# Block-sparse attention feeding a SoLU MLP on one core: mask chain, first columns of Q, spare matmuls and weight loads of the opening rearranged, all priorities set anew

## The chip, the cores and the metric

The kernel runs on one core of a Trainium2 chip. The metric is the device time of one execution in microseconds (us); a kernel's figure is the median of several runs. TensorE is written PE, VectorE DVE, ScalarE ACT, GpSimd POOL, SyncE (which issues most DMAs) SP. Single runs of one and the same kernel here spread by 1 to 1.5% either way. Part of that is PE's clock: in traces of b_rows and of the kernel before, whose instructions up to there are the same, PE came to its full rate at 4.4 and at 16.0 us. Every run therefore comes with the mean clock that was granted to PE.

## The reference, cut to what matters

```python
# q, k, v: (4 batches, 8 heads, 768 tokens, 64); block = 32, so 24 blocks
scores = scale * np.matmul(q, k.transpose(0, 1, 3, 2))
mask = np.abs(blk_i - blk_j) <= 1
mask = mask | (blk_i == 0) | (blk_j == 0) | (blk_i == n_blocks - 1) | (blk_j == n_blocks - 1)
for qb in range(n_blocks):
    for kb in sampled_blocks[qb]:                      # 3 random blocks per row
        mask[qb*32:(qb+1)*32, kb*32:(kb+1)*32] = True
attn = softmax(np.where(mask, scores, -1e9))           # [cut: written out]
x = (attn @ v)                                         # -> (3072 tokens, 512)
h = x @ w_in                                           # (512, 1024)
solu = h * softmax(h)
ln = (solu - mean) / np.sqrt(var + 1e-6) * g_ln
out = ln @ w_out                                       # (1024, 512)
```

## The kernel before

The mask is added inside the score matmul. Rows 64 to 87 of `kT` and `qT` hold a block selector and the block mask, so a score is one matmul over 88 rows, and `exp` of a blocked score is 0. Heads go in pairs; a *unit* is one pair with one query tile of 256: three groups of four score matmuls (one ACT exponential each), then 24 PV matmuls, then a DVE division into `x`. A finished query tile of `x` is transposed by a DMA, multiplied by `w_in`, put through ACT, DVE and POOL, transposed again and multiplied by `w_out`.

All instructions are first put into one list by a planner in the host program: each operation has a priority `due`, and the planner places the ready operation with the smallest one. What comes out is the in-order instruction stream of each engine. So a priority, or an estimated time, that changes in the opening can move every later instruction.

```python
key = (t if late else now, o.due)          # in the planner: earliest, then smallest due
if best is None or key < best[0]:
    best = (key, o, max(t, now))
# [cut]
for i in range(7):                         # 28 spare matmuls for the clock, all at the start
    w = op("PE", 0.43, warm_mm, [m1], due=-60, take="m", after=[w] if i else [])
# [cut: POOL and DVE build selq (24x768), static, anyeq, maskq]
def mask_mm(o):                            # all 768 columns of the mask rows
    for g in range(2):
        nc.tensor.matmul(sbank[o.slot]...[0:NB, g*512 : g*512 + S//2], maskq,
                         selq...[:, g*(S//2) : (g+1)*(S//2)], start=True, stop=True)
# [cut: ACT copies them to qT rows 64..87 of head 0, DVE from there to head 1]
rest = {nm: op("POOL", 0.84, lambda o, t=t: nc.gpsimd.dma_start(      # pairs 1 to 3
    out=t[0][D:DM, 1:NPR]..., in_=t[0][D:DM, 0:1]....broadcast_to([NB, NPR - 1, 2 * S])),
    rows[nm], due=-2059, load=0.8) for nm, t in (("k", kT), ("q", qT))}
w_in_load = op("POOL", 0.82, lambda o: nc.gpsimd.dma_start(
    out=w_in_sb, in_=moe_w_in...), [stage[("k", 0, 2)]], due=-2000, load=6.35)
for i in range(3):                         # w_out in float32, into buffers that are free yet
    w_out_load.append(op("SP", 0.5, lambda o, i=i: nc.sync.dma_start(out=hold[i], ...),
        due=-43.4 + 0.1 * i, load=2.3, after=[stage[("v", 0, 3)]]))
# [cut]
wo = [op("DVE", 0.39, lambda o, c=c: nc.vector.tensor_scalar(         # 8 scalings w_out * g
    out=w_out_sb[:, c, :], in0=w_out_f[c], scalar1=g_sb[:, c:c+1], scalar2=None,
    op0=ALU.mult), [w_out_load[c // 3], gc], due=26) for c in range(KF)]
```

The 24x768 mask rows of the first pair are written once by engines, and then copied to the other three pairs (`rest`) by two POOL DMAs. No `w_out` matmul, and no transpose ahead of one, can start before the eight scalings `wo` are done.

The softmax here doesn't subtract the row's maximum and nothing guards it: scores larger than these inputs give would overflow.

Of the kernel before, what the change touches and what calls it, by code (L numbers as in the profile page):

```python
# [8 lines left out]
BF16 = mybir.dt.bfloat16  # L9
I32 = mybir.dt.int32  # L10
AX = mybir.AxisListType
ALU = mybir.AluOpType
# [3 lines left out]
INF = float("inf")  # L16

# [36 lines left out]
class Plan:  # L54
# [24 lines left out]
    def run(self):  # L79
# [10 lines left out]
        while len(order) < len(self.ops):  # L90
# [17 lines left out]
            self.free[o.eng] = t + o.us  # L108
            o.start = t
            o.seen = t + o.us + SEEN[o.eng]  # L110
# [4 lines left out]
            elif o.load is not None and o.eng != "SP":  # L115
                o.seen = t + 2.8 + o.load + 0.6 * min(o.load, max(0.0, self.dma_free - t - 1.5))
                self.dma_free = max(self.dma_free, t + 1.5) + o.load
            elif o.load is not None:
                self.dma_free = max(self.dma_free, t + 1.0) + o.load
                o.seen = self.dma_free + 1.3  # L120
                self.landed.append(self.dma_free)
                if len(self.landed) > 6:
                    self.free["SP"] = max(t + o.us, self.landed[-7])
# [20 lines left out]
def kernel(  # L144
# [33 lines left out]

    NST, NKB, NEX, NX, NE, NSO, NSOT, NXT, NOT = 4, 3, 9, 6, 2, 3, 3, 2, 3
# [101 lines left out]
    for b in range(B):  # L281
# [6 lines left out]
    m1 = op("DVE", 0.15, lambda o: nc.vector.memset(onesf, 1.0), due=-99)  # L288
    mid = op("POOL", 0.15, lambda o: nc.gpsimd.memset(ident, 0.0), due=-98)
    mids = op("POOL", 0.35, lambda o: nc.gpsimd.affine_select(  # L290
        out=ident, in_=ident, compare_op=ALU.not_equal, fill=1.0, base=0, channel_multiplier=1,
        pattern=[[-1, P]]), [mid], due=-97)

    idf = op("DVE", 0.1, lambda o: nc.vector.tensor_copy(out=identf, in_=ident[0:KF, 0:KF]), [mids], due=-80)

    def warm_mm(o):
        for _ in range(4):
            nc.tensor.matmul(bank(o)[:, 0:P], onesf, onesf, start=True, stop=True)

    for i in range(7):  # L300
        w = op("PE", 0.43, warm_mm, [m1], due=-60, take="m", after=[w] if i else [])
        w.last_of.append((w, "m"))
        w.held["m"][0] = 1


# [6 lines left out]
    def chain(first, steps, due):  # L312
        last = op("POOL", 0.12, first, due=due)
        for us, fn in steps:
            last = op("POOL", us, fn, [last], due=due)
        return last

    def sel(t, us, fill, base, cm, pat, cmp=ALU.is_ge):
# [4 lines left out]
            due=-96)  # L323
    stat = chain(lambda o: nc.gpsimd.memset(static, 0.0),
                 [sel(static, 0.2, -NEG, 1, -1, [[1, NB]]), sel(static, 0.2, -NEG, 1, 1, [[-1, NB]]),
                  sel(static, 0.2, 0.0, -1, 1, [[0, NB]]), sel(static, 0.2, 0.0, NB - 2, -1, [[0, NB]]),
                  (0.1, lambda o: nc.gpsimd.memset(static[:, 0:1], 0.0)),
                  (0.1, lambda o: nc.gpsimd.memset(static[:, NB - 1 :], 0.0))], -94)
    sqs = chain(lambda o: nc.gpsimd.memset(selq, 1.0),
                [sel(selq, 1.05, 0.0, 0, -BLK, [[1, NCH], [NCH, P]]),  # L330
                 sel(selq, 1.05, 0.0, BLK - 1, BLK, [[-1, NCH], [-NCH, P]])], -93)
    last = op("DVE", 0.1, lambda o: nc.vector.memset(anyeq, 0.0), due=-95)
# [8 lines left out]
    def mask_mm(o):  # L341
        for g in range(2):
            nc.tensor.matmul(sbank[o.slot].rearrange("p a b -> p (a b)")[0:NB, g * 512 : g * 512 + S // 2], maskq,
                             selq.rearrange("b c p -> b (c p)")[:, g * (S // 2) : (g + 1) * (S // 2)],
                             start=True, stop=True)

    mmm = op("PE", 0.4, mask_mm, [mq, sqs], due=-2088, take="sh")
    rows = {"k": [], "q": []}
    for hh in range(2):
        rows["k"].append(op("DVE", 0.3, lambda o, hh=hh: nc.vector.tensor_copy(  # L350
            out=kT[0][D:DM, 0, hh, :], in_=selq.rearrange("b c p -> b (c p)")), [sqs], due=-2087 if hh == 0 else -60))
        rows["q"].append(op("ACT" if hh == 0 else "DVE", 0.75 if hh == 0 else 0.3, lambda o, hh=hh: (
            nc.scalar.copy(out=qT[0][D:DM, 0, 0, :].rearrange("p (g n) -> p g n", g=2),
                           in_=sbank[mmm.slot].rearrange("p a b -> p (a b)").rearrange(
                               "p (g n) -> p g n", g=2)[0:NB, :, 0 : S // 2]) if hh == 0 else
            nc.vector.tensor_copy(out=qT[0][D:DM, 0, 1, :], in_=qT[0][D:DM, 0, 0, :])),
            [mmm] if hh == 0 else rows["q"][:1], due=-2087 if hh == 0 else -60,
            last_of=[mmm] if hh == 0 else []))
    rest = {nm: op("POOL", 0.84, lambda o, t=t: nc.gpsimd.dma_start(
        out=t[0][D:DM, 1:NPR].rearrange("p a h q -> p a (h q)"),  # L360
        in_=t[0][D:DM, 0:1].rearrange("p a h q -> p a (h q)").broadcast_to([NB, NPR - 1, 2 * S])),
        rows[nm], due=-2059, load=0.8) for nm, t in (("k", kT), ("q", qT))}
    vones = [op("POOL", 0.15, lambda o, i=i: nc.gpsimd.memset(va[i][:, :, :, D : D + 1], 1.0),
                due=-70 if i == 0 else 0) for i in range(2)]


    w_in_load = op("POOL", 0.82, lambda o: nc.gpsimd.dma_start(
        out=w_in_sb, in_=moe_w_in.rearrange("(c p) f -> p c f", p=P)), [stage[("k", 0, 2)]], due=-2000, load=6.35)
    w_out_load = []
    for i in range(3):  # L370
        w_out_load.append(op("SP", 0.5, lambda o, i=i: nc.sync.dma_start(
            out=hold[i], in_=moe_w_out.rearrange("(c p) d -> p c d", p=P)[:, 3 * i : min(3 * i + 3, KF)]),
            due=-43.4 + 0.1 * i, load=2.3, after=[stage[("v", 0, 3)]]))
    gt = op("PE", 0.1, lambda o: nc.tensor.matmul(bank(o)[:, 0:KF], g8, identf[0:KF, 0:KF], start=True, stop=True),
            [g_load, idf], due=-60, take="m")
    gc = op("DVE", 0.1, lambda o: nc.vector.tensor_copy(out=g_sb, in_=bank(gt)[:, 0:KF]), [gt], due=-60,
# [11 lines left out]
    def prepare(b, pr, due):  # L388
        i = b % 2
        first = b == 0 and pr == 0  # L390
        got = {0: [], 1: []}
        for nm, st, cb, dst in (("k", kst, kb, kT), ("q", qst, qb, qT)):
# [23 lines left out]
            ca = tp0 = None  # L416
            where = "sh" if first else "m"
            at = pair16 if where == "sh" else lambda o: bank(o, BF16)
            for part in range(2 if first else 1):
                cols = slice(part * D, part * D + D) if first else slice(0, P)  # L420
# [13 lines left out]
                def tp(o, at=at, ca=ca, cols=cols, tokens=tokens, tp0=tp0, part=part):  # L434
                    t = at(tp0 or o)[0 : cols.stop - cols.start, part * 1024 : part * 1024 + S]
# [4 lines left out]
                t = op("PE", NCH * 0.056, tp, [c_, mids], due=due, take=None if tp0 else where,  # L440
                       last_of=[ca], after=[tp0] if tp0 else [])
                tp0 = tp0 or t
                for hh in (part,) if first else (0, 1):
                    def cp(o, at=at, dst=dst, hh=hh, tp0=tp0, first=first):
                        r = 0 if first else hh * D
                        d_ = dst[i][0:D, pr, hh, :]
                        s_ = at(tp0)[r : r + D, (1024 * hh if first else 0) : (1024 * hh if first else 0) + S]
                        (nc.scalar.copy if o.eng == "ACT" else nc.vector.tensor_copy)(out=d_, in_=s_)
# [228 lines left out]
```

## Time and profile before

| what | where it is read | value |
|---|---|---|
| time | runs | 217.17 us (216.26 to 218.54) |
| span of the profiled run | page | 216.2 us |
| first score, first exponential | timeline | 8.74, 9.81 us |
| scores wait for the second pair's mask row | timeline | 1.85 us, until 19.05 |
| first `w_in` matmul, first `w_out` matmul | timeline | 45.88, 56.89 us |
| `w_out` scalings on DVE | timeline | 29.57 to 34.2 us |
| full clock from | transposes' durations | 16.0 us |

How to read a timeline line: start, duration, engine, source line, operation, output and input, shapes, how many instructions were merged and, in brackets, how long the engine had been idle and what ended that wait.

### The profile page before, as it was taken

How to read it: one execution, taken by the hardware profiler on the slowest of the kernel's cores; microseconds unless marked ns; L12 is line 12 of the kernel's file. 1: busy time of each engine (PE TensorE's matmuls, PEld its weight loads, DVE VectorE, ACT ScalarE, POOL GpSimd, SP SyncE). 2: the span in 40 equal slices, each digit the busy share in tenths (PEclk: the TensorE clock that was granted, in tenths of full speed). 3: DMA queues.
4: the chain of work that ended last, by engine and by line, in shares of the span. 5: the costliest groups of instructions: out<-in, count | busy, mean ns of one | idle time of the engine just before them, and what ended most of it. 6: DMA issues, size and time to landing. Idle time of an engine off the chain costs nothing.

```text
span 216.2 us, 5660 instructions
## 1 busy us (share of the span) xinstructions
PE 203.1 (94%) x2228; PEld 142.9 (66%) x2228; DVE 152.3 (70%) x358; ACT 164.9 (76%) x198; POOL 63.8 (29%) x135
## 2 busy tenths in 40 slices
PE   7996899899999999999988999999999999999992
PEld 6685787677767767777765677677766555764440
DVE  6554685048495888765965769976687799879991
ACT  3576799969999999999895996999887655934200
POOL 8431011313337063434140632342102211121121
PEclk9997899699999999999999999999999999999999
DMA  5999999997999999998999999995744436705822
GB/s 164 302 254 237 265 395 219 183 235 177 247 243 300 224 188 311 256 303 179 205 210 314 156 279 269 200 184 97 100 107 73 115 97 149 195 5 107 232 97 99
DMA packets 72639, 43.09 MB, mean 199 GB/s; under 512 B 55444, under 2 KB 67740, under 8 KB 72612
## 3 DMA queue, kind: packets, MB, share of 16 engines
q1 hardware_dynamic: 71904, 41.23, 84.2%
q0 software_dynamic: 656, 1.49, 3.5%
q8 instruction: 17, 0.28, 0.6%
q14 instruction: 10, 0.08, 0.1%
q10 hardware_dynamic: 52, 0.00, 0.0%
HBM read 23.07 MB, written 6.29 MB: 136 GB/s over the span
## 4 chain that ended last, share of the span: by engine, by line
PE 64%; DMA 15%; ACT 8%; DVE 5%; SPq 4%; issue 2%; POOL 0%; POOLq 0%; ACTq 0%; DVEq 0%
PE sbank L471 19%; PE mbank L589 16%; PE sbank L543 16%; PE mbank L488 11%; ACT ex L478 8%; DMA qst<-in_q_dram 8%; SPq L265 3%; DMA kb<-kb 3%; DMA qb<-qb 2%; DMA vst<-in_v_dram 2%; PE mbank L518 1%; DVE kT L407 1%; DVE bn L563 1%; DVE eso L556 1%; DVE qT L407 1%
## 5 line engine op out<-in xcount | busy, mean ns | idle before, releaser
L478 ACT ACTIVATE ex<-sbank 128x1024 bf16<-128x1024 f32 x144 | 137.6, 1037 | 14.3 <-PE sbank L471 13.6
L471 PE MATMUL sbank<-qT,kT 88*128 88x256 bf16 x576 | 87.7, 282 | 4.3 <-ACT ex L478 2.1
L471 PEld LDWEIGHTS <-kT 88*128 88x128 bf16 x576 | 54.8, 100 | 29.9 <-issue 7.5
L543 PE MATMUL sbank<-w_in_sb,xT 128*128 128x512 bf16 x192 | 52.5, 379 | 0.0
L488 PEld LDWEIGHTS <-ex 128*128 128x128 bf16 x1152 | 45.5, 100 | 6.2 <-DVE x L502 1.3
L589 PE MATMUL mbank<-w_out_sb,eso 128*128 128x512 bf16 x192 | 48.0, 379 | 1.6 <-DMA eso<-eso 1.1
L488 PE MATMUL mbank<-va,ex 128*128 128x65 bf16 x1152 | 47.3, 196 | 0.8 <-DVE x L502 0.7
L552 ACT ACTIVATE eso<-sbank 128x1024 bf16<-128x1024 f32 x24 | 24.8, 1035 | 21.2 <-issue 11.4
L556 DVE SCALAR_TENSOR_TENSOR eso<-sbank,eso 128x1024 bf16<-128x1024 f32 x24 | 29.3, 1221 | 7.6 <-ACT eso L552 7.5
L563 DVE BATCH_NORM_STATS2 bn<-eso 128x6 f32<-128x512 bf16 x48 | 30.8, 683 | 0.3
L499 DVE RECIPROCAL r<-mbank 128x4 f32<-128x4 f32 x48 | 8.6, 179 | 30.0 <-PE mbank L488 29.5
L589 PEld LDWEIGHTS <-eso 128*128 128x128 bf16 x192 | 17.9, 98 | 17.6 <-DMA eso<-eso 1.2
L570 POOL TENSOR_SCALAR mv<-se,mv 128x1 f32<-128x1 f32 x24 | 6.9, 289 | 76.3 <-DVE mv L566 71.2
L543 PEld LDWEIGHTS <-xT 128*128 128x128 bf16 x192 | 18.0, 98 | 10.1
L599 DVE TENSOR_SCALAR ot<-mbank,rs 128x512 f32<-128x512 f32 x24 | 17.9, 747 | 5.7 <-POOL qb L397 2.3
L502 DVE TENSOR_TENSOR x<-mbank,r 128x256 bf16<-128x256 f32 x48 | 19.9, 415 | 0.9
L454 POOL CAST va<-vst 128x768 bf16<-128x768 f32 x16 | 13.4, 837 | 18.9 <-DMA vst<-in_v_dram 18.9
L574 POOL TENSOR_TENSOR rs<-mv,neg_half 128x1 f32<-128x1 f32 x24 | 13.6, 566 | 12.9 <-DVE ot L599 11.7
L568 POOL TENSOR_TENSOR se<-se 128x1 f32<-128x1 f32 x24 | 4.7, 195 | 28.0 <-ACT eso L552 28.0
L397 POOL CAST kb<-kst 128x768 bf16<-128x768 f32 x12 | 10.2, 853 | 7.8 <-DVE r L499 6.2
L560 DVE TENSOR_SCALAR eso<-eso,mu 128x1024 bf16<-128x1024 bf16 x24 | 11.6, 483 | 0.2
L407 DVE COPY qT<-qb 64x768 bf16<-64x768 bf16 x24 | 10.1, 422 | 2.0 <-DMA qb<-qb 1.7
(64 smaller groups left out, 90.2 us busy)
## 6 DMA issues: line engine op xcount, KB each, us to landing
vst<-in_v_dram SPq DMA_DIRECT2D x16, 384.0 KB, 12.7
out_dram<-ot SPq DMA_DIRECT2D x24, 256.0 KB, 3.7
kst<-in_k_dram SPq DMA_DIRECT2D x15, 384.0 KB, 5.8
qst<-in_q_dram SPq DMA_DIRECT2D x15, 384.0 KB, 4.7
w_in_sb<-in_moe_w_in_dram POOLq DMA_DIRECT2D x1, 1024.0 KB, 13.9
kT<-in_moe_w_out_dram SPq DMA_DIRECT2D x1, 768.0 KB
qT<-in_moe_w_out_dram SPq DMA_DIRECT2D x1, 768.0 KB
eso<-in_moe_w_out_dram SPq DMA_DIRECT2D x1, 512.0 KB
```

Of the source, the lines that this page charges most:

```text
L407: nc.vector.tensor_copy(out=dst[i][0:D, pr, hh, :], in_=half(cb[ca.slot], 1)[hh * D : hh * D + D, :]),
L471: nc.tensor.matmul(s[:, m, :], kT[i][0:DM, pr, hh, jc * P : (jc + 1) * P], qT[i][0:DM, pr, hh, t * TW : (t + 1) * TW], start=(m % 2 == 0), ...
L478: exs.append(op("ACT", act_us(1024), lambda o, so=so: nc.scalar.activation(out=exb[o.slot], in_=sbank[so.slot], func=ACT.Exp, scale=scale) ...
L488: nc.tensor.matmul(acc[:, qt, hh, :], exb[exs[n].slot][:, m, qt * P : (qt + 1) * P], va[i][:, 2 * pr + hh, jc, :], start=(n + m + qt == 0) ...
L502: nrm = op("DVE", 0.39, lambda o: nc.vector.tensor_tensor(out=xb[x_of[(b, t)].slot][:, :, 2 * pr * D : (2 * pr + 2) * D].rearrange("p a (h ...
L543: nc.tensor.matmul(h[:, f * 512 : (f + 1) * 512], xTb[xp.slot][:, a, c, :], w_in_sb[:, c, f * 512 : (f + 1) * 512], start=(c == 0), stop=( ...
L552: se = op("ACT", act_us(d_ff) + 0.22, lambda o, h0=h0: nc.scalar.activation(out=eb[o.slots["e"]], in_=pair(h0), func=ACT.Exp, accum_out=se ...
L556: so = op("DVE", 1.29, lambda o, h0=h0, se=se: nc.vector.scalar_tensor_tensor(out=sob[o.slot], in0=pair(h0), scalar=1.0, in1=eb[se.slots[" ...
L563: bn = op("DVE", 2 * 0.64, lambda o, so=so: [nc.vector.bn_stats(out=bnb[o.slot][:, f], in_=sob[so.slot][:, f * 512 : (f + 1) * 512]) for f ...
L574: rs = op("POOL", 0.55, lambda o, mv=mv: nc.gpsimd.tensor_tensor(out=rsb[o.slot], in0=mvb[mv.slot][:, 0:1], in1=neg_half, op=ALU.pow), [q2 ...
L589: nc.tensor.matmul(bank(o0 or o), sotb[st.slot][:, f, :], w_out_sb[:, f, :], start=(f == 0), stop=(f == KF - 1))
L599: nc.vector.tensor_scalar(out=otb[o.slot], in0=bank(o0), scalar1=rsb[rs.slot], scalar2=None, op0=ALU.mult)
```

## The change

Its intent: start ACT's exponentials earlier and let PE reach and keep its full clock. The mask chain on POOL becomes shorter, by moving memsets to DVE. The mask matmul, the mask-row copies and Q's first copy are split by columns, so that the first query tile (256 columns) does not wait for the rest. Spare matmuls (44 instead of 28) are single ones, to be put into PE's gaps. `w_in` is loaded in two pieces behind the Q of the fourth pair, and `w_out` behind the first piece. All priorities, and some of the planner's estimates, are new.

```diff
-    for i in range(7):
-        w = op("PE", 0.43, warm_mm, [m1], due=-60, take="m", after=[w] if i else [])
+    def warm_mm(o):
+        nc.tensor.matmul(mbank[1][:, 3 * P : 4 * P], onesf, onesf, start=True, stop=True, ...)
+    for i in range(NWARM):                                  # 44
+        op("PE", 0.0535, warm_mm, [m1], due=1e7)
# [cut: memsets from POOL to DVE]
+    mmm = op("PE", 0.11, mask_mm, [mq, sqs], due=-2088, take="sh")        # columns 0..255
+    mmr = op("PE", 0.22, lambda o: mask_mm(o, mmm), [mq, sqs], due=-2079, after=[mmm])
+    qrow = {(0, 0): qrow_op("ACT", 0.36, 0, 0, TW, ps(0, TW), [mmm], -2087, [mmm]),
+            (1, 0): qrow_op("DVE", 0.36, 1, 0, TW, ps(0, TW), [mmm], -2079.6, [mmm])}
+    qrow[(0, 1)] = qrow_op("DVE", 0.62, 0, TW, S, ps(512, 1024), [mmr], -2078, [mmm])
# [cut]
-    w_in_load = op(... out=w_in_sb ..., [stage[("k", 0, 2)]], due=-2000, load=6.35)
+    w_in_load = [op(... out=w_in_sb[:, c : c + 2] ..., [stage[("q", 0, 3)]], due=-2000 + c, load=3.2)
+        for c in (0, 2)]
-            due=-43.4 + 0.1 * i, load=2.3, after=[stage[("v", 0, 3)]]))
+            due=-43.4 + 0.1 * i, load=2.3, deps=w_in_load[:1], after=[stage[("v", 0, 3)]]))
# in prepare(): K and Q of the first head are transposed into one PSUM tile of two banks
+                tp0 = shared_tp if shared and nm == "q" else None
+                off = 1024 if tp0 else 0
# [cut: Q's copies of the first pair split at column 256; new A, F, Q, SHIFT]
```

## The prediction

> **What bounds the kernel now.** I read the page first, then stretches of engine time, then the order of the first 30 us, the DMA issues and the chain of waits. On the page I want the bounding engine and where it is not full.
>
> ```profile
> PE 203.1 (94%) x2228; PEld 142.9 (66%) x2228; DVE 152.3 (70%) x358; ACT 164.9 (76%) x198; POOL 63.8 (29%) x135
> PE   7996899899999999999988999999999999999992
> ACT  3576799969999999999895996999887655934200
> ```
>
> TensorE (PE) is busy for 94% and full nearly everywhere after slice 9 (5.4 us each), so from about 50 us on the kernel is bound by PE. Before that PE's digits flatter it: busy is not full rate. The next view has columns start:end, length, busy time (instructions) of PE, weight loads, DVE, ACT, POOL, then granted clock, DMA share, GB/s.
>
> ```profile
> 9.20:12.60 3.40, 3.40 (x21) 2.59 (x20) 1.55 (x4) 2.05 (x2) 0.62 (x1) 1.00 1.08 275
> 16.00:19.40 3.40, 1.55 (x26) 1.32 (x24) 2.17 (x6) 1.70 (x2) 0.00 (x0) 1.00 1.07 236
> 19.40:22.80 3.40, 3.40 (x28) 2.73 (x26) 1.50 (x3) 2.56 (x3) 0.83 (x1) 0.50 1.11 252
> 36.50:39.90 3.40, 2.40 (x17) 1.54 (x16) 0.30 (x1) 3.40 (x5) 0.83 (x1) 1.00 1.46 134
> 39.90:43.30 3.40, 3.08 (x46) 2.76 (x45) 0.00 (x0) 3.07 (x4) 0.83 (x1) 0.50 0.88 215
> ```
>
> A half-full stretch (16.0 to 19.4, 36.5 to 39.9) is each time followed by one at a clock of 0.50. The column shows 1.00 ahead of 16 us, but the instructions there say otherwise: six transposes take 0.85 us until 15 us and 0.50 us at 16.7. So PE runs at half rate from the start to 16.0 us, and twice more.
>
> The timeline (start, duration, engine, line, operation, count, idle time before it) shows what the first scores wait for:
>
> ```profile
> 3.36 1.17 POOL L319 TENSOR_SCALAR_AFFINE_SELECT selq<-selq 24x768 bf16<-24x768 bf16 x1
> 6.34 0.16 DVE L337 SCALAR_TENSOR_TENSOR maskq<-anyeq,static 24x24 bf16<-24x24 f32 x1
> 6.56 0.81 PE L343 MATMUL sbank<-selq,maskq 24*24 24x384 bf16 x2
> 7.40 0.79 ACT L353 CAST qT<-sbank 24x768 bf16<-24x768 f32 x1
> 8.74 2.74 PE L471 MATMUL sbank<-qT,kT 88*128 88x256 bf16 x12
> 9.81 1.02 ACT L478 ACTIVATE ex<-sbank 128x1024 bf16<-128x1024 f32 x1 [0.81 <-PE sbank L471]
> ...
> 19.05 1.54 PE L471 MATMUL sbank<-qT,kT 88*128 88x256 bf16 x8 [1.85 <-DMA qT<-qT]
> ```
>
> The mask chain (POOL's selects, DVE's maskq, the mask matmuls, ACT's copy of 768 columns, then Q's own copy) releases the first score at 8.74. At 19.05 the second pair of heads waits for its mask row, copied by a POOL DMA that was issued at 10.09. Next, the DMA issues (size, issue to landing) and the longest piece of the chain of waits within the first 60 us:
>
> ```profile
> w_in_sb<-in_moe_w_in_dram POOLq DMA_DIRECT2D x1, 1024.0 KB, 13.9
> qT<-qT POOLq DMA_DIRECT2D x1, 216.0 KB, 8.8
> 8.54 16.96 DMA qst<-in_q_dram
> ```
>
> The Q of the fourth pair is issued at 8.54 and lands at 25.50: w_in, issued at 13.81, is in flight from then to 27.7 and shares the engines with it. The first matmul that uses w_in starts only at 45.88. The chain of attention is late because a weight comes too early.
>
> **What the Trainium skill says.** "TensorE: Matmul & The Clock Gate", Part 1 (The HAM clock gate): the idle state is half rate, and about 3.4 us of sustained work releases it, in windows that do not start with the kernel. The trace agrees: the two 0.50 stretches are 3.4 us long, and full rate comes at 16.0. Part 4 (PE-mode transpose) says that transposes do not count as busy for the gate; that fits a PE that was busy from 5 to 12.6 us and stayed cold, but this trace does not isolate it. "DMA: Bandwidth & Descriptors", Issuing engines are not separate DMA queues: transfers from all queues run on the same 16 engines and interleave; the landing at 25.5 agrees. Same page, Anatomy of one DMA: a POOL DMA costs some 2.0 us plus bytes/436 GB/s, that is 2.5 us for the mask row. The trace differs, 8.8 us, and decides.
>
> **The change part by part.**
>
> *Mask chain.* Four memsets move from POOL to DVE (selq's is 0.73 us on POOL), and POOL runs one short list: iota 0.14, four selects of static at about 0.2, two small memsets at 0.17, ident 0.28, two selects of selq at 0.86 (the undisturbed one): 3.3 us. It starts near 1.1 us, so selq ends at about 4.6, against 4.53 now: no gain there. But static ends near 2.5 instead of 5.52, so maskq comes at about 4.3 instead of 6.50 and the mask matmul is released by selq.
>
> *Column parts.* The first mask matmul has 256 columns, cold about 0.4 us against 0.81. ACT's copies of 256 instead of 768 columns should cost about 0.36 each, estimated from 0.79 for 768 with a third of the columns and a fixed part of 0.15. Chain: 4.7 + 0.4 + 0.2 + 0.36 + 0.36 and handovers gives a first score at about 6.4 to 6.8. I take 6.6, that is 2.1 us earlier. The second score needs the other head of Q, on which ACT waited until 6.75; with cast 0.5, transposes 0.85 and a copy of 0.3 it starts near 8.6. So ACT gets one exponential early and then a gap of about 0.5.
>
> *Spare matmuls.* 44 instead of 28, one by one, without a dependency on each other. Cold ones take 0.107 us, 4.7 us in all, and fill PE from about 1.1 to 6 us or later, interleaved with transposes. I expect full rate somewhere between 6 and 9 us instead of 16.0. Scores before 16 us (24 matmuls, 5.7 us cold) would take 2.6.
>
> *DMA order.* w_in goes behind Q of pair 3 and w_out behind half of w_in. The bulk data up to that Q is 4.3 MB plus 0.4 MB of mask rows; at 164 GB/s for the first 5.4 us (0.89 MB) and then about 275, it lands near 20 us (estimate) instead of 25.5. V of pair 3 follows near 21.5 instead of 27.5. w_in then lands near 30, still ahead of its use.
>
> *Mask row of pairs 1 to 3.* Issued after ACT's and DVE's parts of one head, at about 8 us instead of 10.09; with the same 8.8 us it lands at about 17, not 18.9. The first pair's two units last six exponentials, to about 14. A stall of 1 to 2 us remains unless scores of the third query tile fill it.
>
> *The sum, on ACT's path.* From 9.81 to 42.97 ACT does 31 exponentials. Twelve of them in a row took 11.13 us, 0.93 each, so 31 need 28.8 us; the other 4.4 us were waits. Afterwards: first one at 7.6, 28.8 of work, about 2.0 of waits (0.5 for the second head, 1.5 for the mask row) give 38.4 instead of 43.0: 4.6 us earlier. From there both kernels have the same remaining work, PE-bound, so the shift reaches the end. PE also loses the cold stretch from 39.9 to 43.3 (1.7 us of work), if FFN matmuls fill the gaps between scores that made it; the new priorities put the first w_in matmuls early. I count 1.4 us for that and take off 0.6 for w_in's second half coming later than planned. Gain: 4.6 + 1.4 - 0.6 = 5.4 us, and 217.2 - 5.4 = 211.8.
>
> As a ceiling: up to 50 us PE did 142 score matmuls at 0.109 us, 264 PV matmuls at 0.031, 8 of w_in at 0.216 and eight sets of transposes at 0.34, together 28.1 us of full-rate work, so 21.9 us are lost. With attention bound by ACT from 7.6 to 33 us (PE work of about 2.05 us per unit of three exponentials, 2.8 us), some 13 us of loss cannot go. The most to be had is thus about 9 us.
>
> **The rivals.** *First: the mask row keeps the old rhythm.* The POOL DMA may land at 18 to 19 us anyway, since it is now 144 pieces of half the size. Then pair 1 starts as before, PE idles for over half a window, goes cold again, and only what the earlier loads save later (waits of 0.47, 1.00 and 0.21 us between 21.7 and 28.2) is won, with a little of the filling: about 215. For it speaks the 8.8 us; against it that the second Q part is no longer in its way.
>
> *Second: a transfer takes the place of the one removed.* TensorE executes in order. If w_in or w_out land later than the new order assumes (13.9 us for 1 MB here), the first FFN matmul stands in PE's queue and blocks the scores behind it: 214 to 217. Against it: x of the first query tile is not complete until near 30 us anyway.
>
> *Third: all priorities were set anew.* The full stretch from 60 to 200 us, which now loses only 1.9 us of idle time, may get better or worse by 1 to 3 us, as may the tail, where PE is 4.3 us idle in the last 16. *Fourth: everything works*, FFN work fills PE from 33 us, and 208 to 209 comes out.
>
> **Range and chances.** Centre 211.8; 208.3 to 215.5 should hold it 8 times in 10: the low end is the ceiling of 9 us, the high end the first rival. Faster by over 2% means below 212.8. I give that 0.62, within 2% 0.36, slower 0.02, because nothing on the path gets longer except through the third rival.
>
> **What would show it.** Right: first score near 6.6 us and first exponential near 7.6; six transposes at 0.5 us before 10 us; Q of pair 3 landing near 20; the 31st exponential ending near 38.4; the first w_in matmul well ahead of 45.9; PE full after that. Wrong: a wait on the mask row at 18 us or later; a 0.50 clock stretch between 10 and 25 us; PE waiting on w_in or w_out; a first part that is 5 us earlier with the gain gone at 60 us, or lost between 60 us and the end.

## The result, and the profile after

The changed kernel took 225.52 us (median of 4 runs, 223.30 to 226.68), beside 217.62 us for the kernel before on the same chip (4 runs). It is slower. The ratio is 1.033 (95% interval 1.023 to 1.044). A ratio here is the mean time of one kernel's fast runs over that of the other's fast runs of the same rounds, so it is not quite the ratio of the medians quoted; a run counts as fast when it is within 1.5% of the fastest run of its kernel. A later set of rounds with the unaltered kernel gave 224.28 us and 1.037 (1.032 to 1.042).

On the page of the kernel after, the lines that answer to the first two fences of the prediction are these (busy times, and tenths in 40 slices, here of 5.6 us):

```profile
PE 203.1 (91%) x2216; PEld 142.8 (64%) x2244; DVE 153.7 (69%) x365; ACT 164.5 (74%) x198; POOL 63.6 (29%) x133
PE   6897986899799999999698999999999999999892
ACT  3355997699969998999788989998797467734200
```

The span grew from 216.2 to 222.9 us. That PE is busy for 203.1 us in both says nothing: this trace has 2244 weight loads and only 2216 matmuls, so 28 matmul records are missing from it, and busy time holds stretches at half rate and 16 more spare matmuls. In the complete trace of the same kernel in the last call (after_again), PE is busy for 208.2 of 223.6 us and idle for 15.4, against 13.1 before. So the loss is idle time and half-rate time together. The slices show gaps in the first eleven. (The dip in slice 20 has its like in the two eights of the kernel before, at nearly the same time.)

The opening in the timeline of the kernel after:

```profile
4.88 0.17 DVE L340 SCALAR_TENSOR_TENSOR maskq<-anyeq,static 24x24 bf16<-24x24 f32 x1
...
6.83 0.38 PE L349 MATMUL sbank<-selq,maskq 24*24 24x256 bf16 x1
6.93 0.55 DVE L465 COPY kT<-sbank 64x768 bf16<-64x768 bf16 x1 [1.27 <-PE sbank L452]
...
7.52 0.37 ACT L465 COPY qT<-sbank 64x256 bf16<-64x256 bf16 x1 [1.12 <-DVE kT L465]
...
8.30 0.41 DVE L360 CAST qT<-sbank 24x256 bf16<-24x256 f32 x1 [0.17 <-ACT qT L360]
...
8.77 0.58 PE L349 MATMUL sbank<-selq,maskq 24*24 24x512 bf16 x1 [0.78 <-DVE qT L360]
...
9.28 1.03 PE L500 MATMUL sbank<-qT,kT 88*128 88x256 bf16 x4
...
10.35 1.02 ACT L507 ACTIVATE ex<-sbank 128x1024 bf16<-128x1024 f32 x1 [2.08 <-PE sbank L500]
11.01 0.63 POOL L368 DMA_DIRECT2D qT<-qT  x1 [1.13 <-DVE qT L360]
...
11.02 1.25 PE L307 MATMUL mbank<-onesf 128*128 128x128 bf16 x10
...
12.31 0.28 DVE L465 COPY qT<-mbank 64x256 bf16<-64x256 bf16 x1 [1.97 <-PE mbank L307]
...
12.92 2.77 PE L500 MATMUL sbank<-qT,kT 88*128 88x256 bf16 x12
...
14.01 1.94 ACT L507 ACTIVATE ex<-sbank 128x1024 bf16<-128x1024 f32 x2 [2.64 <-PE sbank L500]
```

Read it as a chain. The inputs of the first mask matmul are ready at 5.05, yet it runs at 6.83, since K's and Q's transposes stand ahead of it in PE's order. DVE's copy of K waits 1.27 us for PE, which is still writing Q's transposes into the same PSUM tile; ACT's copy of Q then waits 1.12 us for DVE's copy of K out of that tile. The mask rows go the same way: ACT reads columns 0 to 255, then DVE, and only then (0.78 us) may PE write the other 512 columns into the tile; that matmul stands in PE's order ahead of the first score. So the first score begins at 9.28, later than the 8.74 of before. Then ten spare matmuls (line 307) run while DVE's copy of Q's second head waits 1.97 us for them, and ACT waits 2.64 us for its second exponential. In the kernel before the second one came at 11.52:

```profile
11.52 1.02 ACT L478 ACTIVATE ex<-sbank 128x1024 bf16<-128x1024 f32 x1 [0.68 <-PE sbank L471]
```

The mask-row DMA is issued at 11.01 instead of 10.09, and its landing decides again (first fence: issue to landing in the kernel after; second: the wait that it ends):

```profile
w_in_sb<-in_moe_w_in_dram POOLq DMA_DIRECT2D x2, 512.0 KB, 12.9
...
qT<-qT POOLq DMA_DIRECT2D x1, 216.0 KB, 9.5
```

```profile
20.65 0.60 PE L500 MATMUL sbank<-qT,kT 88*128 88x256 bf16 x4 [1.38 <-DMA qT<-qT]
```

To see where the loss grows I counted in both traces which scores, PV, `w_in`, `w_out` and transpose matmuls had begun by a given time (by the starts of their weight loads, one for each, since some matmul records are missing), and multiplied by their durations at full rate (0.109, 0.031, 0.216, 0.216 and 0.056 us; an estimate worked out from the traces). The whole is 186.1 us of it in every kernel. The last columns belong to experiments told below; the traced runs of a_wo, a_rows and b_wo_late count as slow (over 1.5% above their fastest), so small differences in their columns mean nothing.

| us of work begun by | before | after | a_wo | a_rows | a_all | b_wo_late | b_rows |
|---|---|---|---|---|---|---|---|
| 15 us | 4.7 | 3.0 | 3.0 | 4.7 | 4.2 | 4.7 | 5.8 |
| 25 us | 10.5 | 9.6 | 10.2 | 13.0 | 12.1 | 9.3 | 13.3 |
| 40 us | 21.3 | 19.7 | 20.1 | 20.3 | 19.7 | 20.7 | 22.5 |
| 50 us | 28.9 | 27.5 | 27.6 | 27.5 | 27.5 | 28.6 | 31.5 |
| 65 us | 43.5 | 38.0 | 40.7 | 38.0 | 40.1 | 37.1 | 46.1 |
| 100 us | 77.8 | 72.6 | 75.0 | 72.5 | 74.4 | 70.0 | 80.4 |
| 200 us | 175.1 | 169.3 | 171.0 | 169.5 | 172.1 | 167.5 | 178.0 |

The kernel after is 1.4 us behind at 50 us, 5.5 at 65 us, and 5.8 at 200 us. So the opening loses a little, and the stretch from 50 to 65 us loses about three times as much (4.1 us). The stretches there, before and then after (columns as in the prediction):

```profile
50.00:58.00 8.00, 7.97 (x112) 6.21 (x111) 5.01 (x16) 7.94 (x9) 2.46 (x4) 1.00 0.91 232
58.00:66.00 8.00, 8.00 (x97) 5.85 (x94) 5.97 (x15) 7.90 (x11) 3.16 (x6) 1.00 1.21 249
```

```profile
50.00:58.00 8.00, 7.42 (x111) 5.74 (x110) 7.67 (x20) 7.93 (x9) 3.05 (x5) 1.00 0.33 81
58.00:66.00 8.00, 6.35 (x51) 4.16 (x53) 4.98 (x12) 6.03 (x8) 2.56 (x5) 0.79 1.05 197
```

In 50 to 58 us DVE is nearly full (7.67 against 5.01), while the DMA engines are a third busy. SyncE's queue, which runs in order, has by then waited 6.9 us for DVE's `x`, ahead of the transpose of `x` that it issues at 54.04, and issues nothing else meanwhile (8.7 us in after_again). In the kernel before no wait of SyncE from 40 to 68 us is longer than 2.5 us. In 58 to 66 us PE has gaps and falls to a mean clock of 0.79, and ACT runs dry with it. What fills DVE, and when the transpose ahead of the first `w_out` matmul and that matmul itself come, the timeline of the kernel after shows; the last fence is the first `w_out` matmul of the kernel before.

```profile
53.93 0.48 DVE L389 TENSOR_SCALAR w_out_sb<-kT,g_sb 128x512 bf16<-128x512 f32 x1
54.32 0.88 DVE L389 TENSOR_SCALAR w_out_sb<-qT,g_sb 128x512 bf16<-128x512 f32 x2
...
55.59 0.70 DVE L389 TENSOR_SCALAR w_out_sb<-qT,g_sb 128x512 bf16<-128x512 f32 x1
56.22 1.44 DVE L389 TENSOR_SCALAR w_out_sb<-eso,g_sb 128x512 bf16<-128x512 f32 x2
```

```profile
57.29 1.23 SPq L611 DMA_TRANSPOSE eso<-eso  x1
```

```profile
57.34 1.24 PE L500 MATMUL sbank<-qT,kT 88*128 88x256 bf16 x8
59.70 0.60 PE L500 MATMUL sbank<-qT,kT 88*128 88x256 bf16 x4 [1.11 <-ACT ex L507]
...
66.95 0.60 PE L618 MATMUL mbank<-w_out_sb,eso 128*128 128x512 bf16 x2
```

```profile
56.89 0.60 PE L589 MATMUL mbank<-w_out_sb,eso 128*128 128x512 bf16 x2
```

The scalings of `w_out` moved from 29.6–34.2 us, when DVE had time, to 48.1–57.7 us. The first `w_out` matmul moved from 56.89 to 66.95 us. In between PE loses time in two ways: ahead of 59.70 it waits 1.11 us for ACT to empty a score buffer (the program has two), and in part of the stretch it runs at half rate. The wait of SyncE isn't made by the scalings alone: in a_wo and a_all, told below, which have them earlier, it is still 6.6 and 6.7 us.

### The profile page after: what moved, and what is told of

It is laid out like the page before. It is cut to its first block, busy times and chain, and to the rows that moved or that the text cites. A ratio compares the mean times of both kernels' runs of the same rounds, so it can differ in the third digit from the quotient of the medians.

```text
span 222.9 us, 5665 instructions
## 1 busy us (share of the span) xinstructions
PE 203.1 (91%) x2216; PEld 142.8 (64%) x2244; DVE 153.7 (69%) x365; ACT 164.5 (74%) x198; POOL 63.6 (29%) x133
## 4 chain that ended last, share of the span: by engine, by line
PE 67%; DMA 18%; DVE 6%; ACT 5%; issue 2%; SPq 0%; DVEq 0%; ACTq 0%
PE sbank L500 20%; PE sbank L572 17%; PE mbank L618 17%; PE mbank L517 11%; DMA kb<-kb 11%; DMA qst<-in_q_dram 6%; ACT ex L507 4%; DVE eso L585 1%; DVE ot L628 1%; DVE kT L419 1%; DMA samp_i<-in_sampled_blocks_dram 1%; PE sbank L452 1%; DVE anyeq L337 1%; DVE x L531 1%; ACT eso L581 1%
## 5 line engine op out<-in xcount | busy, mean ns | idle before, releaser
L507 ACT ACTIVATE ex<-sbank 128x1024 bf16<-128x1024 f32 x144 | 137.6, 1034 | 20.4 <-PE sbank L500 19.7
L517 PEld LDWEIGHTS <-ex 128*128 128x128 bf16 x1152 | 44.8, 98 | 8.4 <-DVE x L531 3.1
L572 PE MATMUL sbank<-w_in_sb,xT 128*128 128x512 bf16 x179 | 48.8, 385 | 1.0 <-ACT ex L507 0.3
L517 PE MATMUL mbank<-va,ex 128*128 128x65 bf16 x1152 | 46.8, 194 | 2.6 <-DVE x L531 2.6
L618 PE MATMUL mbank<-w_out_sb,eso 128*128 128x512 bf16 x177 | 46.0, 379 | 1.9 <-DVE eso L551 0.8
L482 POOL CAST va<-vst 128x768 bf16<-128x768 f32 x16 | 13.3, 831 | 12.1 <-DMA vst<-in_v_dram 12.0
L419 DVE COPY kT<-kb 64x768 bf16<-64x768 bf16 x24 | 8.7, 362 | 10.0 <-DMA kb<-kb 9.8
L409 POOL CAST qb<-qst 128x768 bf16<-128x768 f32 x12 | 10.2, 851 | 7.1 <-DMA qst<-in_q_dram 7.1
```

The lines of the kernel that those rows point to most:

```text
L482: vc = op("POOL", pool_us(S) + 0.3, lambda o: nc.gpsimd.tensor_copy(out=va[i][:, 2 * pr : 2 * pr + 2, :, 0:D], in_=vst[ld.slot]), [ld, von ...
L507: exs.append(op("ACT", act_us(1024), lambda o, so=so: nc.scalar.activation(out=exb[o.slot], in_=sbank[so.slot], func=ACT.Exp, scale=scale) ...
L517: nc.tensor.matmul(acc[:, qt, hh, :], exb[exs[n].slot][:, m, qt * P : (qt + 1) * P], va[i][:, 2 * pr + hh, jc, :], start=(n + m + qt == 0) ...
L572: nc.tensor.matmul(h[:, f * 512 : (f + 1) * 512], xTb[xp.slot][:, a, c, :], w_in_sb[:, c, f * 512 : (f + 1) * 512], start=(c == 0), stop=( ...
L618: nc.tensor.matmul(bank(o0 or o), sotb[st.slot][:, f, :], w_out_sb[:, f, :], start=(f == 0), stop=(f == KF - 1))
```

## The experiments

All eighteen runs gave correct results. Those of the first call let the planner place everything anew; all others move or swap single instructions and keep the order of the rest.

| kernel | what | time (us) | ratio to before (95%) |
|---|---|---|---|
| o_alone | opening and planner constants alone | 233.18 | 1.080 (1.068–1.092) |
| w_alone | weight loads alone | 230.15 | 1.063 (1.053–1.073) |
| p_alone | priorities alone | 228.46 | 1.053 (1.041–1.066) |
| o_and_w | all but the priorities | 230.33 | 1.056 (1.037–1.076) |
| a_nolate | after, without the later spare matmuls | 223.78 | 1.025 (1.020–1.029) |
| a_tiles | and PSUM tiles not shared | 223.53 | 1.023 (1.017–1.028) |
| a_win_early | after, `w_in` earlier | 225.21 | 1.027 (1.018–1.036) |
| b_win_late | before, `w_in` later | 218.07 | 1.001 (0.996–1.007) |
| a_wo | after, scalings earlier | 223.39 | 1.012 (0.996–1.027) |
| a_wo_again | the same | 222.81 | 1.018 (1.009–1.027) |
| b_wo_late | before, scalings later | 223.18 | 1.024 (1.017–1.031) |
| a_rows | a_tiles, second mask row by DVE | 223.34 | none (one fast run) |
| b_rows | before, second mask row by DVE | 214.93 | 0.988 (0.979–0.998) |
| b_rows_win | b_rows and `w_in` later | 215.15 | 0.988 (0.979–0.997) |
| b_rows_again | b_rows | 216.32 | none given |
| after_again | after | 224.28 | 1.037 (1.032–1.042) |
| a_rows_win | a_rows, `w_in` later still | 223.72 | 1.033 (1.027–1.038) |
| a_all | a_rows_win and a_wo | 223.69 | 1.034 (1.029–1.040) |

The kernel before had medians of 218.05, 218.23, 217.42, 217.21 and 218.19 us in the five calls.

**Parts alone, planned anew.** Theory: one part carries the loss. Rival: the priorities, which were searched for one plan, fit only that plan.

```diff
 # o_alone: after, with w_in, w_out and A, F, Q, SHIFT of before
 # w_alone: before, with
+    w_in_load = [op(... w_in_sb[:, c : c + 2] ..., [stage[("q", 0, 3)]], due=-2000 + c, load=3.2) for c in (0, 2)]
+            ... deps=w_in_load[:1] ...                      # w_out
 # p_alone: before, with A, F, Q, SHIFT of after
 # o_and_w: after, with A, F, Q, SHIFT of before
```

> The rebuilt opening alone: new mask chain, column parts, spare matmuls and planner constants; w_in in one piece, w_out and all priorities as in the kernel before. Theory A (the opening itself is the loss: readers and writers of a shared PSUM tile wait for one another, so the first scores come later): slower than before by 1 to 4 us, first score at 9 us or later, second exponential ending near 15. Theory B (the new order of transfers is the loss) and theory C (the new priorities are): within 1 us of before, or faster by up to 2.

> The kernel before with only w_in in two pieces behind Q of the fourth pair and w_out behind its first piece. Theory B: slower by 3 us or more, with scores of the second batch waiting for transposes of K near 35 us. Theories A and C: no slower; the waits on Q and V of the fourth pair go, so up to 4 us faster.

> The kernel before with only the new numbers A, F, Q and SHIFT. Theory C (the priorities, fitted to the planner's idea of the new opening, are the loss): slower by 4 us or more. Theories A and B: within 2 us of before.

> The changed kernel with the old numbers A, F, Q and SHIFT. Theory C: back at the time of before, 216 to 219. Theories A and B: 222 or more, most of the loss stays.

All four are slower than both whole kernels. A part can't be worth minus 15 us and the sum of parts minus 8, so these runs do not apportion the loss: each mix has another order of everything. They support the rival, and they say that in such a kernel a part has to be undone by moving instructions, not by planning anew. (A fifth mix, the changed kernel with the old weight loads, has no run on record.)

**The opening's own waits.** Theory 1: the shared PSUM tiles and the later spare matmuls hold the opening back, and with them gone the predicted gain appears. Rival: the mask-row DMA decides anyway.

```diff
 # a_nolate: only the 26 spare matmuls ahead of the first transposes are kept
+        spares.append(o)
+        if len(spares) > 26:
+            return
 # a_tiles: also K's first transposes in the third score buffer, and
+                if shared and nm == "k":
+                    at = lambda o: sbank[2]...
+    move(mmr, first_score)          # the rest of the mask columns behind the first score
```

> The changed kernel, every engine's order kept, without the 18 spare matmuls that stand after the first score (the first 26 stay). Theory A1 (these spare matmuls share a PSUM bank's tile with Q's second head, whose copy waits for them): the second block of scores starts near 11.5 us instead of 12.9, and if the lead is kept the time is 1 to 1.5 us below the changed kernel. Theory B (transfers bind by 35 us anyway): the lead is there at 15 us and gone by 40 us, time the same. If spare matmuls kept the clock up, the clock is released later than 16.9 and the time is the same or worse.

> As a_nolate, and K's first transposes in the third pair of PSUM banks instead of beside Q's, and the rest of the mask matmul behind the first score instead of ahead of it. Theory A: the copies no longer wait for one another; first score near 7.7 us instead of 9.3, second block near 10, and the time 2 to 4 us below the changed kernel. Theory B: the lead is gone at the scores of the second batch near 36 us, and the time is within 1 us of the changed kernel.

The waits were real. Without the later spares the second block of scores begins at 11.02 instead of 12.92; with separate tiles the first one begins at 8.12. The lines of a_tiles:

```profile
8.12 1.01 PE L507 MATMUL sbank<-qT,kT 88*128 88x256 bf16 x4 [0.73 <-ACT qT L365]
...
10.44 1.44 PE L507 MATMUL sbank<-qT,kT 88*128 88x256 bf16 x6
```

```profile
21.11 1.01 PE L507 MATMUL sbank<-qT,kT 88*128 88x256 bf16 x4 [3.81 <-DMA qT<-qT]
```

But PE then waits 3.81 us for the mask row instead of 1.38, at about the same moment. Both kernels gain about 1% by the ratios against the changed one, and a_tiles (1.023) adds nothing clear to a_nolate (1.025). The rival holds for the lead of the opening: at 21 us it is gone, and by 25 us a_tiles has begun 7.5 us of work and a_nolate 7.6, against 9.6 of the changed kernel. Where the 1% comes from is not shown.

**The order of the loads.** The prediction's largest term came from `w_in` being out of the way of Q. Theory 1: moving `w_in` alone in the kernel before brings most of 4.6 us. Rival: the loads were not what ACT waited for.

```diff
 # b_win_late: before
+    move(w_in_load, ready[(0, 2)][1])      # behind the cast of the third pair's V: issued at 19.6, not 13.8
 # a_win_early: after
+    for o in (w_in_load[1], w_in_load[0]):
+        move(o, ready[(0, 1)][1])          # issued at 12.4, not 17.6
```

> The kernel before with only w_in's issue moved behind POOL's cast of the third pair's V (nothing else moves). The prediction's largest term: Q of the fourth pair lands near 20 us instead of 25.5, the waits of ACT between 21 and 28 us (1.7 us) go, and the time falls by 1.5 to 4 us. Rival: w_in now rides together with the weights and loads that come later, the scores wait elsewhere, and the time is within 1 us of before or above it.

> The changed kernel with only w_in's two issues moved ahead of POOL's cast of the third pair's V, that is issued near 12.5 us instead of 17.6. Theory B (w_in in flight from 22 to 34 us slows the DMA transposes of the second batch's K, issued at 24.7 and landed at 35.1): w_in has landed by 27, those transposes land 3 us or more earlier, and 2 to 3 us are gained by 42 us. Theory A: no change beyond 1 us, or slower, since Q and V of the fourth pair come later.

Q of the fourth pair was cast at 22.49 instead of 25.52, and the waits that the prediction counted are gone. First ACT in the kernel before, from 18 to 30 us, then in b_win_late:

```profile
19.78 1.94 ACT L478 ACTIVATE ex<-sbank 128x1024 bf16<-128x1024 f32 x2 [2.08 <-PE sbank L471]
22.18 1.02 ACT L478 ACTIVATE ex<-sbank 128x1024 bf16<-128x1024 f32 x1 [0.47 <-PE sbank L471]
24.21 3.77 ACT L478 ACTIVATE ex<-sbank 128x1024 bf16<-128x1024 f32 x4 [1.00 <-PE sbank L471]
28.20 1.94 ACT L478 ACTIVATE ex<-sbank 128x1024 bf16<-128x1024 f32 x2 [0.21 <-PE sbank L471]
```

```profile
19.52 11.25 ACT L478 ACTIVATE ex<-sbank 128x1024 bf16<-128x1024 f32 x12 [1.63 <-PE sbank L471]
```

Even so the time is the same: 218.07 against 218.23. The traced run of b_win_late is misleading. It took 214.92 us at a granted clock of 1.000, while its other runs took 217.7 to 219.3 at 0.976 to 0.984; and the kernel before, too, took 214.83 in a run with 0.996. Part of the missing waits is thus the clock: in the trace of before, PE is at half rate from 19.4 to 22.8 us. In the changed kernel an earlier `w_in` changed nothing either (225.21).

**The wait on the mask row.** Theory 1: this wait was the prize in the kernel before, since the stall of PE ahead of 19 us is what sends it to half rate. Rival: the time comes back later.

```diff
 # b_rows: before; the POOL DMA serves pairs 2 and 3, DVE copies the Q rows of pair 1
-        out=t[0][D:DM, 1:NPR]...
+        out=t[0][D:DM, lo:NPR]...           # lo = 1 for K, 2 for Q
+        for hh in range(2):
+            nc.vector.tensor_copy(out=qT[0][D:DM, 1, hh, :], in_=qT[0][D:DM, 0, 0, :])
 # b_rows_win: b_rows with the move of b_win_late;  a_rows: a_tiles with the same two copies
```

> The kernel before with only the Q mask rows of the second pair copied by DVE. Theory E: the wait of 1.85 us at 19.05 goes, PE is not idle in that window, the cold stretch from 19.4 to 22.8 goes too, and the time falls by 1.5 to 3 us. Rival: other transfers (Q of the fourth pair at 25.5) bind next and less than 1 us is left.

> b_rows with w_in's issue moved as in b_win_late. If b_win_late gained nothing because the wait on the mask rows stood ahead of it, the two together gain more than b_rows alone, 3 to 4 us below before. If the loads never bound, the same as b_rows.

> As a_tiles, and the Q mask rows of the second pair copied by DVE on chip instead of by the POOL DMA. Theory E (the lead of a_tiles was lost because the second pair waited to 21.1 us for that DMA): no wait for it, second pair's scores near 17.5, 12 exponentials done before 25 us, and 1.5 to 3.5 us less than a_tiles. Rival: the wait moves to the third pair or to the second batch's transposes and the time stays at that of a_tiles.

> The same kernel as the earlier run: before, with only the second pair's Q mask rows copied by VectorE. If its gain is real: 214.5 to 215.5, ratio 0.985 to 0.992. If the earlier rounds were lucky in the clock's phase: 216 to 218, ratio over 0.995.

In b_rows scores and PV follow one another without a wait where PE stood still before (PE, from 18.4 us):

```profile
18.46 0.60 PE L471 MATMUL sbank<-qT,kT 88*128 88x256 bf16 x4
18.90 0.66 PE L488 MATMUL mbank<-va,ex 128*128 128x65 bf16 x16
19.39 0.60 PE L471 MATMUL sbank<-qT,kT 88*128 88x256 bf16 x4
```

The time is 214.93 us, 1.2% under the kernel before, and the move of `w_in` on top adds nothing (215.15). The repeat is weaker: 216.32 against 218.19, without an interval, because only two of its six runs are within 1.5% of the fastest, 212.27. The twelve runs of b_rows together have a median of 215.4 us. b_rows beats the kernel before by about 1%, on the interval of one call. Its traces show too much: in all three traced runs of b_rows and b_rows_win PE had its full rate from 4.4 to 5.8 us on, against 16.0 in the trace of before, with the same instructions up to there, so part of the lead in the work table is the clock's phase and not the change. The verdict rests on the times of several runs alone.

The changed kernel shows the wait free of that. a_rows and a_tiles both got their full rate at 17 us, and by 25 us a_rows has begun 13.0 us of work, a_tiles 7.5. Yet a_rows takes 223.34 us.

**The late scalings.** Theory 1: the scalings of `w_out` at 48 to 57 us are a cost of their own. Rival: ACT is full there, so they are hidden, and the loss belongs to the later order as a whole.

```diff
 # a_wo: after; scalings in DVE's order behind two divisions and the second pair's K copy, at 44 to 48 us
+    for o, part in zip([*ahead, kcopy], (wo[0:3], wo[3:6], wo[6:8])):
+        for w in reversed(part):
+            move(w, o)
 # b_wo_late: before; scalings where after has them
+    for o, part in zip([kc0, ce0, kc1, nrm], (wo[0:1], wo[1:2], wo[2:5], wo[5:8])):
+        for w in reversed(part):
+            move(w, o)
+    move(so_t, wo[7])                       # the transpose that needs them
+    for o in (mask_rows[("q", 1)], mask_rows[("k", 1)]):
+        move(o, stage[("k", 1, 3)])         # they go into the buffers that hold w_out
```

> The changed kernel with only the eight scalings of w_out moved earlier in DVE's order: three behind the x of 44.2 us, three behind that of 45.6, two at the K copies of 47.4, where DVE is idle and w_out has landed (44.2), instead of 48.1 to 57.2. Theory D (late w_out fills DVE from 50 to 58 us, so x, the transposes behind it on the SP queue and the next loads are late, and PE starves from 58 to 66): DMA share in 50 to 58 well above 0.33, PE above 7.5 of 8 us in 58 to 66, and 2 to 4 us off the changed kernel's time. Rival (the jam only follows the late opening): time within 1 us of the changed kernel.

> The same kernel as the earlier run with the scalings moved to 44 to 48 us, since its first verdict was open. Theory 1 (late scalings cost 2 us): 222 to 223.5, ratio 1.020 to 1.027. Theory 2 (they cost nothing): as the changed kernel, 224 to 225.5, ratio 1.033 to 1.037.

> The kernel before, with only the eight w_out scalings moved in VectorE's order to where the changed kernel has them (48 to 57 us, between the work of the first FFN tile and of the second batch), and with the transpose and the two mask-row copies that depend on them behind; the weight is loaded as early as before, and TensorE's order is the old one. Theory 1 (the late scalings are a cost of their own): the first w_out matmul cannot start before about 60 us instead of 56.9, TensorE waits 2 to 4 us there, and the time is 219.5 to 221.5. Theory 2 (what is lost between 50 and 66 us comes with the changed kernel's whole order, and the place of the scalings is hidden under ScalarE, which is busy throughout 50 to 58 us): within 1 us of the kernel before.

Moved forward in the changed kernel, the scalings give back 1.5 to 2.5% by the ratios (1.012 and 1.018 against 1.033 and 1.037). By the medians above the kernel before of the same call it is 1.1 to 3.3 us (6.0 and 4.6 against 7.9 and 7.1). The ratio of a_wo rests on three fast runs of seven, and its interval includes 1; that of the repeat doesn't. In the work table a_wo is level with after at 50 us and 2.7 us ahead at 65. Moved back in the kernel before, they cost 2.4%, 5.0 us by the medians, more than I expected. Here are PE, and then the stretch from 58 to 66 us, in b_wo_late:

```profile
56.60 0.60 PE L471 MATMUL sbank<-qT,kT 88*128 88x256 bf16 x4
61.91 1.01 PE L589 MATMUL mbank<-w_out_sb,eso 128*128 128x512 bf16 x2 [4.71 <-DMA eso<-eso]
```

```profile
58.00:66.00 8.00, 4.09 (x35) 2.98 (x36) 2.80 (x7) 2.20 (x4) 1.74 (x3) 0.63 0.71 156
```

The first `w_out` matmul keeps its place in PE's order, so PE stands still for 4.71 us until the transpose behind the scalings has landed, and then runs cold (0.63). The work table shows 28.6 us begun by 50 us against 28.9, and 37.1 by 65 us against 43.5. (The traced run is one of the two slow ones, 225.68 us, so only its order and its waits are used here.) The rival is refuted where it says "hidden": late scalings, with the transpose and the two mask-row copies that have to move with them, cost the kernel before 2.4%, while the changed kernel loses 3.3 to 3.7%. It is not an exact share of the loss, since the changed kernel had put the matmul later and avoids the full stall. The rival's other half, a loss from the later order, stands beside it: of the 4.1 us lost from 50 to 65 us, a_wo gets back 2.6.

**The mends together.** Theory 1: the mends add up, to about the time of before or better. Rival: a later wait in the new order takes what each one wins.

```diff
 # after_again: none.   a_rows_win: a_rows, and
+    for w in reversed(w_in_load):
+        move(w, casts[1])                   # behind the casts of the second batch's first K and Q
 # a_all: a_rows_win, with the move of a_wo
```

> The changed kernel once more, unaltered, so that the two below have it on the same chip. Every theory: 1.02 to 1.045 of before.

> a_rows with w_in's two issues moved behind POOL's casts of the second batch's first K and Q. Theory B1 (w_in, in flight from 22 to 31 us, makes the DMA transposes of that K and Q late, and DVE, in order, stands before their copies from 29.4 to 33 us): transposes land 2 to 4 us earlier, the wait of 3.6 us shrinks below 1.5, the lead over the changed kernel is still there at 40 us and the time is 2 to 3 us below a_rows. Rival B2 (the loads themselves and the order of the SP queue set it, not w_in): the wait stays near 3.6 us, or w_in, now landing after 40 us, holds up the first FFN matmuls at 46; time as a_rows or above.

> a_rows_win with the scalings of w_out moved as in a_wo. If the loss of the changed kernel is the three waits found so far (opening, second batch's transposes, DVE jam behind the late w_out), they add up: 218 or less, the time of before. If the order of its later part is itself worse, 220 to 222 is left.

They do not add up: 223.72 and 223.69. The longest waits of a_all between 28 and 40 us on the path of the scores (us in total, times, longest), and the stretch from 30 to 38 us in a_all and then in before:

```profile
DVE qT L424 <- DMA qb<-qb: 4.7, 1, 4.7
...
PE sbank L507 <- DVE qT L424: 4.5, 1, 4.5
```

```profile
30.00:38.00 8.00, 3.43 (x43) 2.58 (x42) 2.20 (x7) 3.72 (x5) 1.00 (x2) 0.78 1.11 255
```

```profile
30.00:38.00 8.00, 7.20 (x114) 5.79 (x111) 5.25 (x16) 8.00 (x10) 0.99 (x2) 1.00 1.11 266
```

The new order has the second batch's first scores at about 35 us in the streams of PE and DVE, ahead of other work. They need Q of that batch, transposed by DMA, and in a_all that lands at 35.67, 11.3 us after its issue at 24.40. The kernel before issues the same transpose at 41.42 and uses it at 50.10, in a place where PE has FFN work meanwhile. So whatever the opening wins is lost at this wait: 12.1 us of work by 25 us, 19.7 by 40 us, the same as the changed kernel. What delays the transpose is not isolated. The move of `w_in` is no test of `w_in`: in a_all its first half is issued at 24.32, 0.08 us ahead of this transpose (24.40), and its second half lands at 35.32, 0.34 us ahead of it. K's transpose, which goes ahead of `w_in` there, lands at 28.5 in a_all and 30.2 in a_rows_win, against 33.0 in a_rows. In the kernel after and in a_win_early K's transpose lands 0.7 us after the load of K that was issued ahead of it (34.40 and 34.34, then 35.05), though in a_win_early `w_in` had landed at 28.2. In other traces the distance is up to 2 us. This points to the backlog of loads issued ahead of a transpose, `w_in` one of them; no run takes that backlog away. Why a_all shows nothing of what a_wo gave back stays open as well; by the ratios it is clear (1.034 against 1.012 and 1.018), by the medians it is only 0.5 to 1.9 us (6.5 above the kernel before, against 6.0 and 4.6).

## Why the prediction was wrong

The range was 208.3 to 215.5 us, and "slower by over 2%" had a chance of 0.02. By the prediction's own steps:

- **Column parts, first score at 6.6.** Wrong: 9.28. The durations were about right (ACT's copies took 0.37 and 0.36 us, estimated 0.36 each). The step left out two things. One is PE's order: the mask matmul, planned for 4.7, had its inputs at 5.05 and ran at 6.83, behind the transposes of K and Q. The other is who shares a PSUM tile: waits of 1.27, 1.12 and 0.78 us. The Trainium skill, "PSUM — Partial Sum Buffer", Terms, has two engines on one bank of the same quadrant of partitions at once as an error, so such accesses must be kept apart in time. For the spare matmuls and Q's second head this is the case, one bank, and the trace agrees with 1.97 us. K's and Q's transposes lie in two different banks of one tile; there the program's own dependencies made the waits, and a_tiles, which separates them (and also moves the rest of the mask columns), starts the first score at 8.12, which is 1.16 of the 2.7 us.
- **Spare matmuls, full rate between 6 and 9.** Wrong in this trace: 16.9 us, before 16.0. The spares do not decide it alone: with the very same early spares b_rows had its full rate by 4.9 us and b_win_late at 16.4. In a_wo_again, with the opening of the changed kernel, it came at 5.3 us and was lost again from about 8.6 to 15.3, so the later spares did not keep it. Their number was not varied by itself. The later spares cost the 1.9 us that a_nolate takes away.
- **Mask row, issued at about 8, landing near 17.** Wrong: issued at 11.01, landing at about 20.5. This is the first rival, and worse than it, since the rows of both column parts have to be there before the DMA. The prediction had this wait in view and left it in the sum with 1.5 us. b_rows shows that it was the place to look.
- **DMA order, the 4.6 us on ACT's path.** The mechanism as far as the landing was right: Q of the fourth pair landed at 20.98 in the kernel after (predicted near 20, before 25.50). But DVE's order cast it only at 25.02, against 25.52 before, and the 31st exponential, due near 38.4, ended at 47.60. The inference from a wait in one trace to the time was wrong: b_win_late has the waits removed and 0.1% to show for it. Two readings in the sum were off as well: 42.97 is the end of the 30th exponential (the 31st ends at 45.27), and by 50 us PE had done ten sets of transposes and not eight, so the ceiling starts from 28.8 us of work and 21.2 lost. Neither explains the miss.
- **"From there both kernels have the same remaining work, PE-bound, so the shift reaches the end."** This is the step that failed most, and in sign: the path did get longer after the opening. `w_out` behind `w_in` was booked as free, with 0.6 us for `w_in`'s second half alone, although eight DVE scalings hang on it. They ran at 48 to 57 us, the first `w_out` matmul came 10 us later, and between 50 and 65 us the kernel fell from 1.4 to 5.5 us behind. a_wo and b_wo_late show the cost of the scalings from both sides. They are not the whole of it: SyncE's wait of 6.9 us for `x` in the same stretch stays at 6.6 in a_wo. The second rival had the kind of trouble (a transfer that comes late and PE in order) but named the wrong consumer: the matmuls' wait for the load, not DVE's work between them.
- **Third rival, new priorities: 1 to 3 us either way between 60 and 200 us.** The late stretch itself was undisturbed: the gap is 5.2 us at 100 and 5.8 at 200 us. The trouble was before 66 us. And a_all shows that the order of the new plan is part of it, with the second batch's scores at 35 us waiting for a transpose.
- **"Nothing on the path gets longer except through the third rival."** This sentence gave the 0.02, and it was the worst one: the first score, the second exponential, the end of the mask-row wait and the first `w_out` matmul all came later, by 0.5, 2.5, 1.6 and 10 us.

How the 7 to 8 us divide is thus only bounded: 1.1 to 3.3 us by the medians (1.5 to 2.5% by the ratios) for the late scalings, about 1% for the opening's later spare matmuls, and the rest in the new order, where SyncE waits for `x`, the second batch's scores wait for a transpose, and the mends replace one another's waits. That rest was not isolated.

## What to carry to other kernels

When a load moves, follow it to its last consumer: here the load of a weight was harmless, and eight small DVE instructions behind it, moved from a slack stretch into a full one, were worth 1.5 to 2.5%. Before counting on a split by columns, look whether the parts share a PSUM tile, and what stands ahead of the first part in an in-order engine: here the two together took more than the split was to gain. The short stall that ended on a slow DMA swallowed here what was won ahead of it; take such a one away first (here two DVE copies of 24 rows, about 1%), and test parts of a planned kernel by moving instructions, not by planning anew.

## What the Trainium skill lacked or had wrong

- "DMA: Bandwidth & Descriptors", Anatomy of one DMA: worked out from its fit, a 216 KB mask row from POOL is estimated at 2.5 us. It took 8.8 and 9.1 us before, 9.5 after, and 8.3 for 144 KB in b_rows, while other loads were under way. The page has no figure for such a load on a busy chip.
- "TensorE: Matmul & The Clock Gate", Part 1: it puts the first release about 4 us into sustained matmul work, ±0.5 us from run to run. For an opening that has gaps, as here, that can't be carried over. With the same 24 to 28 spare matmuls from 1.1 us on, full rate came between 4.4 and 4.9 us in b_rows, at 16.0 in before, 16.4 in b_win_late and 16.9 in after.
- No page gives the time from issue to landing of a DMA transpose among other loads, only a bandwidth: here 11.3 us in a_all (24.40 to 35.67), and 3.3 us in the kernel before (41.42 to 44.69).
- "PSUM — Partial Sum Buffer" tells of one bank. It has nothing on a program that keeps engines apart by whole tiles of two banks, which cost 1.27 and 1.12 us here.
